# Two sequences transformed inside SBUF instead of one, and full-width transfers in the first stage

## The chip, the cores and the metric

One core of one Trainium2 chip runs the whole program: TensorE (PE) for matmuls and transposes, VectorE (DVE), ScalarE (ACT), GpSimd (POOL), and SyncE (SP), which only issues transfers here. The metric is the device time of one execution in microseconds; lower is better. Runs of the kernel before gave 543.24, 546.17 and 552.6 us.

## What is computed

Eight sequences of 2496 rows and 256 channels pass a real Fourier transform along the rows, are multiplied by a complex filter per frequency and channel, and are transformed back. The 19968 rows that result go to a mixture of eight experts with 80 places each: a row's expert is the one with the largest logit, each expert keeps the 80 rows with the largest gate, and all other output rows are zero.

```python
X = np.fft.rfft(x, axis=1)
y = np.fft.irfft(X * (filt_r + 1j * filt_i)[None], n=2496, axis=1).reshape(19968, 256)
logits = y @ w_gate                       # 8 experts
expert, gate = argmax(logits), softmax(logits)[expert]
for e in range(8):                        # the 80 rows of e with the largest gate
    out[rows_e] = gate[rows_e] * (relu(y[rows_e] @ w1[e]) @ w2[e])
```

## The kernel before, in words

The length is split as 2496 = 39 x 64: row number 64 n1 + n2. **Stage 1** is a transform over n1 (39 points, of which 20 frequencies s are kept, real and imaginary), one small matmul with the table `wf_t`. Three sequences share a matmul: 3 x 39 = 117 partitions go in, 120 come out. Two forms of it exist.

- The **near** form (`stage1_near`, L363) takes one sequence, sequence 0, whose 64 values of n2 are laid into three parts of 22, 22 and 20, one part per block of 39 partitions. Its chunks (`CHUNKS`, six of them, four values of n2 in each part, the last with two) are loaded as three transfers of 39 partitions. It uses x as the stationary side, so the result has channels on partitions; ACT and DVE copy it into a tile `u`, and `turn_near` (L388) transposes it into the form that stage 2 wants. Nothing goes through DRAM.
- The **far** form (`stage1`, L330) takes a trio of sequences, 1 to 3 and then 4 to 6 (`TRIOS`), in 16 chunks of four values of n2. ACT copies the result to `t1` and stores it on its own transfer queue to a DRAM tile `d1`; `load_t2` (L355) reads it back in the other layout, five loads per sequence. Sequence 7, alone, uses the same route with the chunks of the near form and three small stores per chunk. A trio chunk's x is loaded as 112 and 5 partitions.

**Stage 2** (`stage2`, L401) runs in steps: a step is two frequencies s of one sequence, ten steps per sequence, 80 in all. It transforms over n2 (eight instructions on PE with the table `d_t`), DVE multiplies by the two filter planes `ft`, POOL forms the complex sum. Two steps later (`LATE`) `turn` (L424) transposes the result with the gate weights beside it; ACT copies it out, DVE reduces the gate part. Spectra of sequences 0, 1, 2 and 7 stay in SBUF (`KEEP`), the others go to DRAM in `yf`, through a ring of two `ysp` tiles and POOL's queue. The filter planes are loaded as rows (`load_filter`, L280) and transposed on PE (`turn_filter`, L290) in five groups during sequence 0, each group with a part of `d_t`.

The order is written out by hand (from L786): `plan` says after which part of which step a piece runs. `chunk()` runs one stage-1 chunk and first issues the load of the chunk four places on. Before step 0 the six near chunks of sequence 0 run; the first trio's 16 chunks lie in steps 0 to 7, the second trio's in steps 10 to 34, sequence 7's in steps 60 to 65. The loads of `t2` for a sequence stand one sequence ahead, those of sequence 1, 4 and 7 in the last steps. From step 42 on, logits, gating and a first selection (`logits_e`, `logits`, `gating`, `first_pick`) of sequences 0 to 5 are placed in between. SP's queue is in order, and each of its transfers also waits for a free completion slot, of which the eight are used in turn by SP and ACT.

After step 81 come the **rows out**: for each sequence, in the order `ORDER`, the table rows of up to 128 selected positions are gathered (`fetch`), transposed in five groups and multiplied with that sequence's spectrum (`turn_rows`, `rows_out`). Spectra in DRAM are loaded into two buffers (`spectrum`). `aside` places other pieces by group number, 40 groups in all. Then the experts run on the 640 rows. `put_zeros` writes the zeros of the output, 26 transfers in all: in steps 40 to 61, in ten of the groups, and eight in the expert stage, which the planner may place earlier since nothing there is written out by hand.

The stationary table of the far form and its load:

```python
wf_t = tpool.tile([NP1, NM1], F32, name="wf_t")          # 117 x 120
for p0, np_ in ((0, 112), (112, NP1 - 112)):             # load_x, trio
    nc.sync.dma_start(out=xt[p0:p0 + np_], ...)
```

Of the kernel before, what the change touches and what calls it, by code (L numbers as in the profile page):

```python
# [29 lines left out]

H3, J3 = 3, 22
# [3 lines left out]
TRIOS = (1, 4)  # L35
# [11 lines left out]
ORDER = (0, 1, 2, 3, 4, 5, 6, 7)  # L47
# [3 lines left out]
def dft_tables():  # L51
# [27 lines left out]
    return (wf.reshape(NP1, NM1).astype(f32), v.transpose(2, 0, 1).astype(f32),  # L79
# [5 lines left out]
def kernel(  # L85
# [14 lines left out]
    wf_host, wi_host, d_host, e_host, rows_host = dft_tables()  # L100
    wf_dram = nc.inline_tensor(wf_host, name="wf_tbl")
    wi_dram = nc.inline_tensor(wi_host, name="wi_tbl")
# [131 lines left out]
    with ExitStack() as fctx, tc.manual_schedule():  # L234
# [19 lines left out]
        wf_t = tpool.tile([NP1, NM1], F32, name="wf_t")  # L254
# [5 lines left out]
        ft = [tpool.tile([128, NS, NDB, NQ], F32, name=f"ft{i}") for i in range(2)]  # L260
# [3 lines left out]
        def load_tables(part):  # L264
            if part == 0:
                nc.scalar.dma_start(out=wf_t, in_=wf_dram.ap())
# [23 lines left out]
        def turn_filter(k, g):  # L290

            ps = fps.tile([128, SG, NDB, NQ], F32, name=f"pf_{k}_{g}", tag="f")
            for i in range(SG):
                for cb in range(NDB):
                    nc.tensor.transpose(ps[:, i, cb, :],
                                        fst[k, g][0:NQ, i, 128 * cb:128 * cb + 128],
                                        ident[0:NQ, 0:NQ])
            nc.vector.tensor_copy(out=ft[k][:, SG * g:SG * g + SG], in_=ps[:])
# [3 lines left out]
        def load_x(b, ch, trio=False):  # L302
            if trio:
                xt = xpool.tile([128, JC, C], F32, name=f"x_{b}_{ch}", tag="x")
                for p0, np_ in ((0, 112), (112, NP1 - 112)):
                    nc.sync.dma_start(
                        out=xt[p0:p0 + np_],
                        in_=bass.AP(tensor=x.tensor,
                                    offset=x.offset + (b * S + N2 * p0 + JC * ch) * C,
                                    ap=[[N2 * C, np_], [C, JC], [1, C]]))  # L310
                st["x", b, ch] = xt
                return
            j0, jn = CHUNKS[ch]
            xt = xpool.tile([128, JC, C], F32, name=f"x_{b}_{ch}", tag="x")

            def rows(p0, np_, j1, jm, row):
                nc.sync.dma_start(
                    out=xt[p0:p0 + np_, j1:j1 + jm, :],
                    in_=bass.AP(tensor=x.tensor, offset=x.offset + row * C,
                                ap=[[N2 * C, np_], [C, jm], [1, C]]))  # L320

            for h in range(H3):
                r0 = b * S + J3 * h + j0
                if b == B - 1 and h == H3 - 1 and J3 * h + j0 + jn > N2:
                    rows(N1 * h, N1 - 1, 0, jn, r0)
                    rows(N1 * h + N1 - 1, 1, 0, jn, B * S - jn)
                else:
                    rows(N1 * h, N1, 0, jn, r0)
            st["x", b, ch] = xt

        def stage1(b, ch, trio):
# [6 lines left out]
            j0, jn = (JC * ch, JC) if trio else CHUNKS[ch]  # L338
# [7 lines left out]
            if trio:  # L346
                nc.scalar.dma_start(out=st["d1w", b][:, j0:j0 + jn, :], in_=t1[:, 0:jn, :])
                return
            for h in range(H3):
                n0 = J3 * h + j0  # L350
                jm = min(jn, N2 - n0)
                if jm > 0:
# [437 lines left out]
        for b in TRIOS:  # L790
            xs += [(b, ch, True) for ch in range(NTC)]
# [689 lines left out]
```

## Time and profile before

| | |
|---|---|
| median of three runs | 546.17 us (543.24 to 552.6) |
| the profiled execution | 544.47 us, span 542.7 us, mean granted TensorE clock 0.906 |
| PE matmuls | 458.3 us, 84% of the span |
| DVE, POOL, ACT | 202.4, 175.2, 154.6 us |
| moved by DMA | 135.92 MB, mean 250 GB/s |
| queue of SP and ACT (q1, q10) / POOL (q0) | 53.0% and 10.0% / 12.0% of 16 engines |

The span is the time from the first to the last instruction; the 1.8 us beside it lie around the program. Busy shares are means over stages with different limits, so the rows further down are taken by stretch and from the instructions in order of time. A timeline row gives the start, the length, the engine, the line, the operation, how many instructions it merges, and in brackets how long the engine had stood idle and what ended that. A granted clock of 1.00 is 2.4 GHz; a stretch with less is a mean over the two levels, 1.2 and 2.4.

### The profile page before, as it was taken

Reading aid. Unit: us, or ns where it says so; the run is one execution under the profiler, and the core shown is the slowest. Engines: PE = TensorE matmul, PEld = TensorE weight load, DVE = VectorE, ACT = ScalarE, POOL = GpSimd, SP = SyncE. Lnnn points to the kernel's source line nnn. Section 1 sums busy time; section 2 is a strip of 40 time slices with the busy share of each in tenths; the row PEclk is TensorE's granted clock in tenths of the full one; section 3 lists DMA queues with packets and bytes.
Section 4 is the critical chain, followed back from the end, with each engine's and each line's share of the span. In section 5 each row is a group of like instructions: output and inputs, shape, how many; then the busy total and the mean of one; then the engine's idle time right before and its main releaser. Section 6 shows DMA issues by size and latency. Waiting matters only on the chain. (4 is left out here: it accounts for less than half of the span.)

```text
span 542.7 us, 7821 instructions
## 1 busy us (share of the span) xinstructions
PE 458.3 (84%) x2845; PEld 378.6 (70%) x2845; DVE 202.4 (37%) x516; ACT 154.6 (28%) x292; POOL 175.2 (32%) x257
## 2 busy tenths in 40 slices
PE   5397797799999989979977877998998796599993
PEld 5374554678878879868846776876887685588882
DVE  4042312354554544887226897036350000001110
ACT  1133342244444224533344121342322121001110
POOL 4010221344454654577324456011025000401111
PEclk9788989899999989999898897798999888569997
DMA  7978989799989797999943600978558987949400
GB/s 207 202 176 264 286 224 325 233 370 327 332 296 306 239 385 260 374 364 382 324 166 130 229 39 7 403 274 298 175 190 284 401 294 229 337 171 320 169 13 13
DMA packets 71671, 135.92 MB, mean 250 GB/s; under 512 B 5445, under 2 KB 54085, under 8 KB 69961
## 3 DMA queue, kind: packets, MB, share of 16 engines
q1 hardware_dynamic: 60180, 92.98, 53.0%
q0 software_dynamic: 6144, 23.95, 12.0%
q10 hardware_dynamic: 5300, 18.41, 10.0%
q8 instruction: 25, 0.41, 0.3%
q14 instruction: 22, 0.17, 0.1%
HBM read 82.68 MB, written 52.64 MB: 249 GB/s over the span
## 5 line engine op out<-in xcount | busy, mean ns | idle before, releaser
L419 POOL TENSOR_TENSOR yt<-p,p 128x256 f32<-128x256 f32 x80 | 61.2, 764 | 187.8 <-PE py L431 104.5
L414 DVE TENSOR_TENSOR p<-pb,ft 128x512 f32<-128x512 f32 x160 | 102.6, 683 | 22.3 <-PE pb L407 19.7
L431 PEld LDWEIGHTS py<-gi,yt 128*128 128x128 f32 x640 | 88.5, 204 | 26.9 <-issue 15.5
L431 PE MATMUL py<-gi,yt 128*128 128x136 f32 x640 | 95.3, 295 | 11.8 <-POOL yt L421 9.1
L407 PE MATMUL pb<-d_t,t 128*128 128x128 f32 x640 | 90.1, 286 | 3.5 <-DMA t<-d 2.3
L407 PEld LDWEIGHTS pb<-d_t,t 128*128 128x128 f32 x640 | 82.0, 200 | 7.8 <-issue 6.1
L343 PE MATMUL pa<-x,wf_t 117*120 117x512 f32 x150 | 76.8, 643 | 9.3 <-DMA x<-in_x_dram 9.0
L345 ACT COPY t<-pa 120x512 f32<-120x512 f32 x75 | 42.8, 586 | 71.9 <-PE pa L343 51.7
L421 POOL TENSOR_TENSOR yt<-p,p 128x256 f32<-128x256 f32 x80 | 58.8, 735 | 0.0
L456 DVE TENSOR_REDUCE z<-py 128x16 f32<-128x32 f32 x80 | 15.0, 188 | 116.1 <-ACT yk L453 75.5
L343 PEld LDWEIGHTS pa<-x,wf_t 117*120 117x120 f32 x150 | 27.3, 199 | 36.3 <-issue 23.6
L941 PE MATMUL po<-yb,wt 128*128 128x256 f32 x160 | 40.4, 398 | 5.5 <-DMA yb<-yf 4.5
L941 PE MATMUL po<-yk,wt 128*128 128x256 f32 x160 | 39.9, 396 | 1.3 <-ACT wt L929 1.3
L453 ACT COPY ysp<-py 128x512 f32<-128x512 f32 x40 | 23.0, 584 | 62.2 <-DMA yf<-ysp 32.8
L929 ACT COPY wt<-pw 128x512 f32<-128x512 f32 x40 | 23.3, 586 | 55.5 <-PE pw L928 55.3
L941 PEld LDWEIGHTS po<-yb,wt 128*128 128x128 f32 x160 | 30.4, 201 | 9.7 <-issue 4.9
L1060 PEld LDWEIGHTS ph<-xs,w 128*128 128x128 f32 x256 | 36.1, 227 | 1.1 <-DVE xs L1056 0.5
L1060 PE MATMUL ph<-xs,w 128*128 128x80 f32 x256 | 36.1, 311 | 0.3 <-DVE xs L1056 0.3
L453 ACT COPY yk<-py 128x512 f32<-128x512 f32 x40 | 23.4, 585 | 43.8 <-PE py L431 40.3
L941 PEld LDWEIGHTS po<-yk,wt 128*128 128x128 f32 x160 | 30.4, 200 | 5.2 <-ACT wt L929 1.6
L1074 PE MATMUL po<-w,hT 128*80 128x256 f32 x128 | 31.3, 394 | 0.0
L1056 DVE COPY xs<-px 128x160 f32<-128x160 f32 x8 | 2.5, 323 | 72.5 <-PE px L1053 72.5
(164 smaller groups left out, 393.5 us busy)
## 6 DMA issues: line engine op xcount, KB each, us to landing
out_dram<-zero_t SPq DMA_DIRECT2D x26, 768.0 KB
t<-d SPq DMA_DIRECT2D x35, 512.0 KB
w<-in_moe_w_dram SPq DMA_DIRECT2D x16, 1024.0 KB
d<-t ACTq DMA_DIRECT2D x32, 480.0 KB
x<-in_x_dram SPq DMA_DIRECT2D x32, 448.0 KB
yf<-ysp POOLq DMA_DIRECT2D x20, 512.0 KB
yb<-yf SPq DMA_DIRECT2D x4, 2560.0 KB
x<-in_x_dram SPq DMA_DIRECT2D x30, 156.0 KB
```

The source lines that it names most:

```text
L343: nc.tensor.matmul(out=ps[0:NM1], lhsT=wf_t, rhs=xt[0:NP1, 2 * i:2 * i + 2, :], start=True, stop=True)
L345: nc.scalar.copy(out=t1[:, 2 * i:2 * i + 2, :], in_=ps[0:NM1])
L407: nc.tensor.matmul(out=ps[:, i, cb], rhs=d_t[:, s, :], start=True, stop=True, lhsT=st["t2", b, s // SG][:, s % SG, 128 * cb:128 * cb + 128])
L414: nc.vector.tensor_tensor(out=pt, in0=ps[:].rearrange("p s c r q -> p (s c) r q"), in1=f.unsqueeze(2).to_broadcast([128, 2 * NDB, 2, NQ]), ...
L419: nc.gpsimd.tensor_tensor(out=yt[:, :, 0, :], in0=pr[0][:, :, 0, :], in1=pr[1][:, :, 1, :], op=AL.subtract)
L421: nc.gpsimd.tensor_tensor(out=yt[:, :, 1, :], in0=pr[0][:, :, 1, :], in1=pr[1][:, :, 0, :], op=AL.add)
L431: nc.tensor.matmul(out=ps[:, i, 136 * cb:136 * cb + 136], rhs=gi[:, cb, :], lhsT=yt[:, 2 * i + cb].rearrange("p r q -> p (r q)"), start=Tr ...
L453: nc.scalar.copy(out=ys[:, m:m + 2, :].rearrange("p i (k c) -> p i k c", k=NDB), in_=ps[:, :, 0:288].rearrange("p i (k c) -> p i k c", k=N ...
L929: nc.scalar.copy(out=wts[t][:, SG * g:SG * g + SG, :], in_=ps[:])
L941: nc.tensor.matmul(po, lhsT=wts[t][:, s, :], rhs=yk[b][g][:, m, :], start=(s == 0), stop=(s == NS - 1))
L1060: nc.tensor.matmul(ph[:, fc // 4, fc % 4, 0:cap], lhsT=w1s[e][:, k, 128 * fc:128 * fc + 128], rhs=xs[:, k, :], start=(k == 0), stop=(k == ...
L1074: nc.tensor.matmul(po[0:cap, :], lhsT=hT[:, fc, :], rhs=w2s[e][:, fc, :], start=(fc == 0), stop=(fc == NFC - 1))
```

## The change

- Sequences 0 and 1 both take the near form; the trios are 2 to 4 and 5 to 7. The far form for one sequence is gone. The chunks of sequence 1 lie in steps 0 to 5, its transposes (`turn_near`) in steps 9, 11, 13, 15 and 17; the first trio's chunks in steps 5 to 15, the second's in steps 20 to 44.
- The first stage's transfers: a near part takes every third partition (0, 3, ... or 1, 4, ... or 2, 5, ...) with a table `wn_t` in that order. A trio chunk is one load over 128 partitions, whose first eleven belong to the sequence before and meet zero rows in the table (now 128 x 128); the store is 128 partitions wide, into a DRAM tile padded to 64 frequencies.
- Both filter planes are loaded into one tile of 128 partitions and transposed together; a group is 8 transposes of 128 x 128 instead of 16 of 64.
- The start: five chunks ahead instead of four, ahead of the filters and `d_t`; the third part of sequence 0's chunks goes to ACT's queue. A chunk's load is issued after the chunk that frees its buffer.
- Rows out in the order 0, 3, 1, 4, 2, 5, 6, 7, with the loads of spectra 5 and 6 at groups 10 and 20 (20 and 25 before).
- Zeros: 14 in steps 50 to 76, six in the groups, six in the expert stage.

```diff
--- before.py
+++ after.py
...
-TRIOS = (1, 4)
+TRIOS = (2, 5)
...
-ORDER = (0, 1, 2, 3, 4, 5, 6, 7)
+ORDER = (0, 3, 1, 4, 2, 5, 6, 7)
...
-    return (wf.reshape(NP1, NM1).astype(f32), v.transpose(2, 0, 1).astype(f32),
+    wt = np.zeros((128, 128))
+    wt[128 - NP1:, :NM1] = wf.reshape(NP1, NM1)
+    wn = wf.transpose(1, 0, 2, 3, 4).reshape(NP1, NM1)
+    return (wt.astype(f32), wn.astype(f32), v.transpose(2, 0, 1).astype(f32),
...
-        wf_t = tpool.tile([NP1, NM1], F32, name="wf_t")
+        wf_t = tpool.tile([128, 128], F32, name="wf_t")
+        wn_t = tpool.tile([NP1, NM1], F32, name="wn_t")
...
-        ft = [tpool.tile([128, NS, NDB, NQ], F32, name=f"ft{i}") for i in range(2)]
+        ft = tpool.tile([128, 2, NS, NDB, NQ], F32, name="ft")
...
+                nc.scalar.dma_start(out=wn_t, in_=wn_dram.ap())
                 nc.scalar.dma_start(out=wf_t, in_=wf_dram.ap())
...
-        def load_filter(k, g):
-            fst[k, g] = t2pool.tile([128, SG, C], F32, name=f"fst_{k}_{g}", tag="t2")
-            filt = (filt_r, filt_i)[k]
+        def load_filter(g):
+            fst[g] = t2pool.tile([128, SG, C], F32, name=f"fst_{g}", tag="t2")
             for q in range(2):
-                off, step = (0, C) if q == 0 else (N1 * C, -C)
+                for k, filt in enumerate((filt_r, filt_i)):
+                    off, step = (0, C) if q == 0 else (N1 * C, -C)
+                    nc.sync.dma_start(
+                        out=fst[g][64 * k + 32 * q:64 * k + 32 * q + 32],
+                        in_=bass.AP(tensor=filt.tensor, offset=filt.offset + off + step * SG * g,
+                                    ap=[[N1 * C, 32], [step, SG], [1, C]]))
+        def turn_filter(g):
+            for i in range(0, SG, 2):
+                ps = fps.tile([128, 2, NDB, 2, NQ], F32, name=f"pf_{g}_{i}", tag="f")
+                for m in range(2):
+                    for cb in range(NDB):
+                        nc.tensor.transpose(ps[:, m, cb].rearrange("p k q -> p (k q)"),
+                                            fst[g][:, i + m, 128 * cb:128 * cb + 128], ident[:])
+                s = SG * g + i
+                nc.vector.tensor_copy(
+                    out=ft[:, :, s:s + 2].rearrange("p k s c q -> p (s c) k q"),
+                    in_=ps[:].rearrange("p s c k q -> p (s c) k q"))
...
+        def load_x(b, ch, trio):
+            xt = xpool.tile([128, JC, C], F32, name=f"x_{b}_{ch}", tag="x")
+            st["x", b, ch] = xt
+            if trio:
+                row = b * S - N2 * (128 - NP1) + JC * ch
                 nc.sync.dma_start(
-                    out=fst[k, g][32 * q:32 * q + 32],
-                    in_=bass.AP(tensor=filt.tensor, offset=filt.offset + off + step * SG * g,
-                                ap=[[N1 * C, 32], [step, SG], [1, C]]))
...
-        def load_x(b, ch, trio=False):
-            if trio:
-                xt = xpool.tile([128, JC, C], F32, name=f"x_{b}_{ch}", tag="x")
-                for p0, np_ in ((0, 112), (112, NP1 - 112)):
-                for p0, np_ in ((0, 112), (112, NP1 - 112)):
-                    nc.sync.dma_start(
...
             j0, jn = CHUNKS[ch]
-            xt = xpool.tile([128, JC, C], F32, name=f"x_{b}_{ch}", tag="x")
...
-            def rows(p0, np_, j1, jm, row):
...
+            for h in range(H3):
+                row = b * S + J3 * h + j0
+                q = nc.scalar if b == 0 and h == H3 - 1 else nc.sync
+                q.dma_start(
+                    out=xt[h:NP1:H3, 0:jn, :],
                     in_=bass.AP(tensor=x.tensor, offset=x.offset + row * C,
-                                ap=[[N2 * C, np_], [C, jm], [1, C]]))
...
+                                ap=[[N2 * C, N1], [C, jn], [1, C]]))
...
+        def stage1(b, ch):
             if ch == 0:
-                n = H3 if trio else 1
-                d1 = d1pool.tile([n * NS, 2 * N2, C], F32, name=f"d1_{b}")
-                for i in range(n):
+                d1 = d1pool.tile([64, 2 * N2, C], F32, name=f"d1_{b}")
+                d1 = d1pool.tile([64, 2 * N2, C], F32, name=f"d1_{b}")
+                for i in range(H3):
...
-            t1 = t1pool.tile([NM1, JC, C], F32, name=f"t1_{b}_{ch}", tag="t1")
-            for i in range(jn // 2):
+            t1 = t1pool.tile([128, JC, C], F32, name=f"t1_{b}_{ch}", tag="t1")
+            for i in range(JC // 2):
                 ps = fps.tile([128, 2, C], F32, name=f"pa_{b}_{ch}_{i}", tag="f")
-                nc.tensor.matmul(out=ps[0:NM1], lhsT=wf_t, rhs=xt[0:NP1, 2 * i:2 * i + 2, :],
+                nc.tensor.matmul(out=ps, lhsT=wf_t, rhs=xt[:, 2 * i:2 * i + 2, :],
                                  start=True, stop=True)
-                nc.scalar.copy(out=t1[:, 2 * i:2 * i + 2, :], in_=ps[0:NM1])
...
-            for h in range(H3):
-                n0 = J3 * h + j0
-                jm = min(jn, N2 - n0)
-                if jm > 0:
-                    nc.scalar.dma_start(out=st["d1w", b][:, n0:n0 + jm, :],
-                                        in_=t1[2 * NS * h:2 * NS * h + 2 * NS, 0:jm, :])
+                nc.scalar.copy(out=t1[:, 2 * i:2 * i + 2, :], in_=ps)
+            nc.scalar.dma_start(out=st["d1w", b][:, JC * ch:JC * ch + JC, :], in_=t1)
...
-        def stage1_near(ch):
...
-                st["u"] = keep_a.tile([128, NDB, NS, 2, N2], F32, name="u", tag="ka")
-            xt = st.pop(("x", 0, ch))
+                st["u", b] = keep_a.tile([128, NDB, NS, 2, N2], F32, name=f"u_{b}", tag="ka")
+            xt = st.pop(("x", b, ch))
...
-                                     lhsT=xt[0:NP1, j, 128 * cb:128 * cb + 128], rhs=wf_t,
+                                     lhsT=xt[0:NP1, j, 128 * cb:128 * cb + 128], rhs=wn_t,
...
-        def turn_near(g):
-            t2 = t2pool.tile([128, SG, C], F32, name=f"t2_0_{g}", tag="t2")
-            u = st["u"].rearrange("p k s r n -> p k s (r n)")
+        def turn_near(b, g):
+            t2 = t2pool.tile([128, SG, C], F32, name=f"t2_{b}_{g}", tag="t2")
+            u = st["u", b].rearrange("p k s r n -> p k s (r n)")
...
-        xs = [(0, ch, False) for ch in range(len(CHUNKS))]
+        todo = [(b, ch, False) for b in range(TRIOS[0]) for ch in range(len(CHUNKS))]
         for b in TRIOS:
-            xs += [(b, ch, True) for ch in range(NTC)]
-        xs += [(B - 1, ch, False) for ch in range(len(CHUNKS))]
-        todo = list(xs)
+            todo += [(b, ch, True) for ch in range(NTC)]
+        NX1 = 5
         def chunk():
-            if len(todo) > 4:
-                load_x(*todo[4])
-            b, ch, trio = todo.pop(0)
-            if b == 0:
-                stage1_near(ch)
+            b, ch, trio = todo[0]
+            if trio:
+                stage1(b, ch)
             else:
-                stage1(b, ch, trio)
-
-        for i in range(4):
+                stage1_near(b, ch)
+            if len(todo) > NX1:
+                load_x(*todo[NX1])
+            todo.pop(0)
+        for i in range(NX1):
             load_x(*todo[i])
-        load_d(0)
         for t in range(B, B + NX):
             nc.gpsimd.dma_start(out=y_sel[128 * t:128 * t + 128, :], in_=zero_t[:, 0:C])
         def ahead(g):
             if g < NS // SG:
-                if g:
-                    load_d(g)
-                for k in range(2):
-                    load_filter(k, g)
+                load_filter(g)
+                load_d(g)
...
+        for i in range(len(CHUNKS)):
+            put(i, 1, chunk)
         for i in range(NTC):
-            put(i // 2, 1, chunk)
-            put(NU + 25 * i // NTC, 1, chunk)
-        for i in range(len(CHUNKS)):
-            put(NU * NA + i, 1, chunk)
-
-        for b in range(1, B):
+            put(5 + 11 * i // NTC, 1, chunk)
+        for i in range(NTC):
+            put(2 * NU + 26 * i // NTC, 1, chunk)
+        for g in range(NS // SG):
+            put(NU - 1 + 2 * g, 2, part(turn_near, 1, g))
+        for b in range(2, B):
             for g in range(NS // SG):
-                u = 8 + (g > 2) if b == 1 else 2 * g
-                if b in (TRIOS[1], B - 1):
-                    u = 7 + (g > 2) + (g > 3)
-                put(NU * (b - 1) + u, 2, part(load_t2, b, g))
+                put(NU * (b - 1) + (8 + (g > 2) if b in TRIOS else 2 * g), 2, part(load_t2, b, g))
...
-        for i in range(8):
-            put(NU * 4 + 3 * i, 2, part(put_zeros, 1))
+        for i in range(14):
+            put(NU * 5 + 2 * i, 2, part(put_zeros, 1))
         ahead(0)
+        chunk()
         ahead(1)
-        for ch in range(len(CHUNKS)):
+        for ch in range(1, len(CHUNKS)):
             chunk()
         for g in range(NS // SG):
-            turn_near(g)
-            for k in range(2):
-                turn_filter(k, g)
+            turn_near(0, g)
+            turn_filter(g)
             ahead(g + 2)
             step(2 * g)
             step(2 * g + 1)
...
-        aside.setdefault(20, []).append(lambda: spectrum(5))
-        aside.setdefault(25, []).append(lambda: spectrum(6))
+        aside.setdefault(20, []).append(lambda: spectrum(6))
+        aside.setdefault(10, []).append(lambda: spectrum(5))
         aside.setdefault(30, []).append(lambda: load_weights(0))
         aside.setdefault(35, []).append(lambda: load_weights(1))
-        for i in range(10):
-            aside.setdefault(4 * i + 1, []).append(lambda: put_zeros(1))
+        for i in (3, 7, 12, 15, 22, 26):
+            aside.setdefault(i, []).append(lambda: put_zeros(1))
...
-        put_zeros(3 if e < 4 else NZ)
+        put_zeros(2 if e < 4 else NZ)
```

## Rows read from the trace of the kernel before

**Rows 1.** Windows: stretch, its us, PE PEld DVE ACT POOL busy, PEclk, DMA share, GB/s.
```profile
6.00:30.00 24.00, 14.96 (x87) 14.68 (x88) 4.83 (x20) 3.42 (x15) 0.53 (x2) 0.82 0.96 222
30.00:108.00 78.00, 64.26 (x338) 42.46 (x337) 23.91 (x44) 25.98 (x47) 14.08 (x20) 0.90 0.83 251
108.00:190.00 82.00, 81.46 (x537) 65.48 (x537) 41.75 (x86) 34.63 (x60) 41.27 (x60) 1.00 0.95 312
253.00:291.00 38.00, 34.30 (x194) 25.48 (x194) 12.34 (x30) 15.35 (x29) 11.47 (x18) 0.87 0.67 235
340.00:360.00 20.00, 19.69 (x116) 16.09 (x116) 0.95 (x2) 7.49 (x14) 0.61 (x1) 0.83 0.99 400
```

**Rows 2.** Timeline, SP then PE, start: start us, us, engine, line, operation.
```profile
16.84 4.25 SPq L317 DMA_DIRECT2D x<-in_x_dram  x6
...
14.65 2.02 PE L372 MATMUL pn<-wf_t,x 117*128 117x120 f32 x16 [0.63 <-DMA x<-in_x_dram]
...
24.99 5.45 PE L372 MATMUL pn<-wf_t,x 117*128 117x120 f32 x24 [8.33 <-DMA x<-in_x_dram]
...
33.21 1.16 PE L407 MATMUL pb<-d_t,t 128*128 128x128 f32 x8
```

**Rows 3.** Timeline of PE, steps 4 and 8.
```profile
67.00 6.39 PE L343 MATMUL pa<-x,wf_t 117*120 117x512 f32 x8 [3.10 <-DMA x<-in_x_dram]
...
99.37 1.69 PE L407 MATMUL pb<-d_t,t 128*128 128x128 f32 x8 [1.17 <-DVE t L396]
```

**Rows 4.** Timeline of PE at the full clock, single kinds of work.
```profile
79.40 1.04 PE L393 MATMUL pt<-ident,u 128*128 128x128 f32 x8
...
170.44 1.88 PE L343 MATMUL pa<-x,wf_t 117*120 117x512 f32 x4
...
180.26 1.05 PE L407 MATMUL pb<-d_t,t 128*128 128x128 f32 x8
...
182.08 1.05 PE L407 MATMUL pb<-d_t,t 128*128 128x128 f32 x8
```

**Rows 5.** Timeline of PE, stage 2 of steps 10, 40, 50, 60, 70.
```profile
107.20 1.13 PE L407 MATMUL pb<-d_t,t 128*128 128x128 f32 x8 [2.31 <-DMA t<-d]
...
190.33 1.05 PE L407 MATMUL pb<-d_t,t 128*128 128x128 f32 x8
...
222.78 1.06 PE L407 MATMUL pb<-d_t,t 128*128 128x128 f32 x8
...
253.18 1.05 PE L407 MATMUL pb<-d_t,t 128*128 128x128 f32 x8
...
305.22 2.08 PE L407 MATMUL pb<-d_t,t 128*128 128x128 f32 x8
```

**Rows 6.** The page's DMA issues: what, queue, count, KB of each.
```profile
out_dram<-zero_t SPq DMA_DIRECT2D x26, 768.0 KB
...
t<-d SPq DMA_DIRECT2D x35, 512.0 KB
...
d<-t ACTq DMA_DIRECT2D x32, 480.0 KB
...
x<-in_x_dram SPq DMA_DIRECT2D x32, 448.0 KB
...
yf<-ysp POOLq DMA_DIRECT2D x20, 512.0 KB
...
x<-in_x_dram SPq DMA_DIRECT2D x30, 156.0 KB
```

**Rows 7.** Timeline of ACT and its queue, steps 40 and 62.
```profile
193.10 1.07 ACT L453 COPY ysp<-py 128x512 f32<-128x512 f32 x2 [6.38 <-DMA yf<-ysp]
...
265.78 3.84 ACTq L353 DMA_DIRECT2D d<-t  x3
```

**Rows 8.** Busy time by stretch, steps 56 to 61.
```profile
240.00:260.00 20.00, 16.23 (x104) 13.87 (x103) 15.85 (x37) 7.26 (x14) 14.31 (x21) 0.91 1.04 372
```

**Rows 9.** Timeline of PE in the rows-out stage.
```profile
432.20 3.75 PE L941 MATMUL po<-yb,wt 128*128 128x256 f32 x8 [3.90 <-DMA yb<-yf]
```

More of the change, by code (lines that the diff above doesn't have):

```diff
@@ L98 @@
     assert 1 <= cap <= 128
-    wf_host, wi_host, d_host, e_host, rows_host = dft_tables()
+    wf_host, wn_host, wi_host, d_host, e_host, rows_host = dft_tables()
     wf_dram = nc.inline_tensor(wf_host, name="wf_tbl")
+    wn_dram = nc.inline_tensor(wn_host, name="wn_tbl")
     wi_dram = nc.inline_tensor(wi_host, name="wi_tbl")
@@ L290, in turn_filter @@
[L290 to L298, printed above, removed]
-        st, zt = {}, {}
-        def load_x(b, ch, trio=False):
-            if trio:
-                xt = xpool.tile([128, JC, C], F32, name=f"x_{b}_{ch}", tag="x")
-                for p0, np_ in ((0, 112), (112, NP1 - 112)):
-                    nc.sync.dma_start(
[L307 to L311, printed above, removed]
+                for k, filt in enumerate((filt_r, filt_i)):
[4 more added lines that the diff above has]
+                                    ap=[[N1 * C, 32], [step, SG], [1, C]]))
@@ L312, in load_x @@
+        st, zt = {}, {}
+        def load_x(b, ch, trio):
[3 more added lines that the diff above has]
+                row = b * S - N2 * (128 - NP1) + JC * ch
+                nc.sync.dma_start(
+                    out=xt, in_=bass.AP(tensor=x.tensor, offset=x.offset + row * C,
+                                        ap=[[N2 * C, 128], [C, JC], [1, C]]))
                 return
             j0, jn = CHUNKS[ch]
-            xt = xpool.tile([128, JC, C], F32, name=f"x_{b}_{ch}", tag="x")
@@ L316, in rows @@
-            def rows(p0, np_, j1, jm, row):
-                nc.sync.dma_start(
-                    out=xt[p0:p0 + np_, j1:j1 + jm, :],
-                    in_=bass.AP(tensor=x.tensor, offset=x.offset + row * C,
-                                ap=[[N2 * C, np_], [C, jm], [1, C]]))
-            for h in range(H3):
[L323 to L328, printed above, removed]
@@ L344, in stage1 @@
                                  start=True, stop=True)
-                nc.scalar.copy(out=t1[:, 2 * i:2 * i + 2, :], in_=ps[0:NM1])
[L346 to L349, printed above, removed]
-                n0 = J3 * h + j0
-                jm = min(jn, N2 - n0)
-                if jm > 0:
-                    nc.scalar.dma_start(out=st["d1w", b][:, n0:n0 + jm, :],
-                                        in_=t1[2 * NS * h:2 * NS * h + 2 * NS, 0:jm, :])
+                nc.scalar.copy(out=t1[:, 2 * i:2 * i + 2, :], in_=ps)
@@ L381, in stage1_near @@
                         n0 = J3 * h + j0
-                        copy(out=st["u"][:, cb, :, :, n0:n0 + jm].rearrange(
+                        copy(out=st["u", b][:, cb, :, :, n0:n0 + jm].rearrange(
                                  "p s r j -> p (s r) j"),
                              in_=ps[:, 0:jm, h].rearrange("p j s r -> p (s r) j"))
-        def turn_near(g):
-            t2 = t2pool.tile([128, SG, C], F32, name=f"t2_0_{g}", tag="t2")
-            u = st["u"].rearrange("p k s r n -> p k s (r n)")
+        def turn_near(b, g):
+            t2 = t2pool.tile([128, SG, C], F32, name=f"t2_{b}_{g}", tag="t2")
+            u = st["u", b].rearrange("p k s r n -> p k s (r n)")
             for i in range(0, SG, 2):
-                ps = fps.tile([128, 2, C], F32, name=f"pt_{g}_{i}", tag="f")
+                ps = fps.tile([128, 2, C], F32, name=f"pt_{b}_{g}_{i}", tag="f")
                 for m in range(2):
@@ L396, in turn_near @@
                 copy(out=t2[:, i:i + 2, :], in_=ps[:])
-            st["t2", 0, g] = t2
+            st["t2", b, g] = t2
         NU = NS // 2
@@ L412, in stage2 @@
                 pt = ppool.tile([128, 2 * NDB, 2, NQ], F32, name=f"p{k}_{b}_{u}", tag=f"p{k}")
-                f = ft[k][:, 2 * u:2 * u + 2].rearrange("p s c q -> p (s c) q")
+                f = ft[:, k, 2 * u:2 * u + 2].rearrange("p s c q -> p (s c) q")
                 nc.vector.tensor_tensor(
```

6 lines of the change are left out of this document (2 added, 4 removed).

## The prediction

> **What bounds the kernel now.** I read the stretches first, then TensorE's instructions in order of time, then the transfers. TensorE (PE) is the engine that every stage passes through, and the table of stretches shows where it isn't fed: busy 15.0 of 24 us in 6 to 30, 64.3 of 78 in 30 to 108, but 81.5 of 82 in 108 to 190 [rows 1]. In the first two the 16 DMA engines show a share of 0.96 and 0.83 while they move only 222 and 251 GB/s; in 340 to 360 the same share moves 400 [rows 1]. So the front (near stage of sequence 0, and steps 0 to 9) is held by loads, the middle by PE. What the reader should see in the start: SyncE (SP) issues the fifth x chunk at 16.84, behind filters and tables in its queue, and PE stands 8.33 us until 24.99 [rows 2]. In steps 0 to 9 the same happens in small, 3.10 us before the row at 67.00, and the eight matmuls behind it take 6.39 us on the lower of the clock's two levels (1.2 for 2.4 GHz; 0.90 granted on the mean of 30 to 108, 1.00 at 108 to 190) [rows 1, 3]; four at the upper level take 1.88 [rows 4]. Step marks are the rows of stage 2: step 0 at 33.21 [rows 2], 10 at 107.20, 40 at 190.33, 50 at 222.78, 60 at 253.18, 70 at 305.22 [rows 5].
>
> **Prices on PE at full clock.** A bare step (stage 2 and a turn) is 182.08 - 180.26 = 1.82 us; a trio chunk is 1.88, of which 0.17 lies under the next instruction (its neighbours' overlap), so 1.71; eight 128-wide transposes 1.04 [rows 4]; sixteen near instructions 2.02, so the 88 of a sequence at most 11.1, and 10 taken [rows 2].
>
> **The start.** The new order puts five x chunks ahead of the filters, one third on ACT's queue. The 8.33 wait goes, and the 24 instructions behind it run at the pace of the sixteen (3.0 us for 5.45): -10.7. Late next is the sixth chunk, behind the first filters and d_t group: some 3.5 MB (15 loads of 156 KB, tables, one filter and table group of 0.8 MB, three small loads), 12 to 16 us at 300 to 222 GB/s from about 3 us on. That is 15 to 19, when PE is at its fifth chunk, so at worst 2 us stay. ACT issues seven transfers before its first copy; its queue is held for some 4 us while it has nothing to copy. Taken: -10, ends -8 and -11; step 0 at 23.
>
> **Steps 0 to 9** (74.0 us now). Half of the first trio's chunks leave; the second near stage comes. PE work: 16.4 (nine full steps' worth, as the first two have no turn), 8 chunks 13.7, near 10, six groups of near transposes 6.2, five filter groups 5.2 (eight wide transposes each in place of sixteen narrow ones; DVE's ten copies keep their size): 51.5. For x still late I add 4, between 0 and the excess of now: that is 74 less the work of the present plan, 16.4 + 16 x 1.71 + 5 x 1.04 twice, so 20. Four is taken since the bytes ask for less: 13 trio chunks of 0.52 MB, 8 stores of 0.52, x of sequence 1 at 2.5, three filter and table groups 2.4, together 16 MB [rows 6], 288 GB/s over 55.5 us. -19; ends -22 and -10. DVE and ACT gain six near chunks' copies; they are busy 24 and 26 of 78 us in this stretch [rows 1], so these lie beside PE (without that cover some 0.9 us per chunk).
>
> **Steps 10 to 39** (83.1 now). 30 x 1.82 = 54.6, 21 chunks 35.9, four near transposes 4.2. The near t2 of sequence 1 is made right ahead of the step that uses it; the same pattern shows 1.17 us of waiting on DVE's copy [rows 3], five times 5.9 (between 0 and 1.3 each). Sum 100.6: +17.5. Load here: 19 x chunks, 21 stores, 15 t2 loads, four yf stores of 0.52 MB and one 1.3 MB table, 32.3 MB, 321 GB/s; 108 to 190 moved 312 at a share of 0.95 [rows 1, 6]. So transfers and PE are about level: at 312 it would be 103.5 (+20), at 400 PE alone is left.
>
> **What the wider transfers give.** Each trio load becomes one of 512 KB over 128 partitions for 448 and 20 KB, each store 512 for 480 [rows 6]: 2.4 MB more in all. The near loads are spread in steps of three partitions. The nearest rows for their pace are 222 GB/s (39 neighbouring partitions each) and 400 (full width) [rows 1]; I take 300 to 330. The Trainium skill (SBUF — State Buffer, "Door 1: The DMA port swizzle") says that a transfer's bandwidth follows how many of 16 ports its partitions reach; 39 neighbours reach about half of them, the step of three all, and the 222 beside 400 agrees. Against the change speaks a rule of DMA: Bandwidth & Descriptors ("Why a DMA increments its semaphore by 16 and not by 1"): the split goes over the largest divisor up to 16, so 39 partitions use 13 engines. By that, near loads stop at 13/16 of 400, 325 GB/s, and 5 MB take 3 us more than at full width; no row here shows it alone.
>
> **Steps 40 to 49** (32.4 now): three chunks come, 5.1; the first zero write moves away from step 40, where ACT waited 6.38 us for a yf store [rows 7] and PE lost about 4. +1, ends -3 and +5. **Steps 50 to 59** (30.4): DVE is busy 15.9 of 20 us there [rows 8] with gating and products; untouched, 0.
>
> **Steps 60 to 69** (52.0 now). Sequence 7's own first stage goes: 11 matmuls of 512 columns, 5.5 chunks, 9.4 us; 17 stores on ACT's queue (by the loop), of which three held its queue 3.84 us [rows 7] with the turn's and the logits' copies behind them; PE idled 3.7 of 38 us there and its clock was granted at 0.87 [rows 1], some 5 us lost. So -9.4 at least, -18 at most. Late next is DVE's gating chain of sequences 4 and 5. -14.
>
> **Zeros.** All 26 writes of 768 KB [rows 6] stay; fourteen now lie in steps 50 to 76, and the planner may set the tail's six beside them. With yf and t2 of these steps that is 26 MB in about 80 us, 325 GB/s: hidden by DVE's steps while the yf stores keep their share; t2 behind them on SP has ten steps of room. 0, between -3 and +10 (rival two).
>
> **Rows out.** The order 0, 3, 1, 4, 2 frees the two buffers of loaded spectra earlier, so the loads of 5 and 6 start about 10 and 5 groups sooner. The 3.90 us wait for yb goes, and the eight matmuls behind it take 1.9 for 3.75 [rows 9]: -6. Spectrum 3 is needed about 15 us after its load starts, 5 MB ahead of or beside it at 400 GB/s: 13 us, hidden barely; if not, +2. The tail of experts is unchanged.
>
> **Sum:** -10 - 19 + 17.5 + 1 - 14 - 6 = -30.5 from the profiled execution's 544.47 us (span 542.7): 514. The median of the runs is 546.17, 1.7 above it: **515.5** for a median.
>
> **Rivals.** One: the full width moves no more than the present one, and the front stays bound by transfers at the 251 GB/s of now throughout. Then steps 0 to 9 take 16/0.251 = 64 and 10 to 39 32.3/0.251 = 129 us: 37 over my sum, 552, no change. For it: the share of 0.83 to 0.96 in the whole front; against it: 312 with the same kinds of transfer at 108 to 190 [rows 1]. At 290 GB/s it is 525, inside my range. 0.12. Two: zeros queued with yf make ACT wait for its yf buffer, as at 193 [rows 7]; if half of the ten stores of sequences 5 and 6 cost 4 us, or if the planner sets the tail's six zeros (4.7 MB, 15 us) in steps 20 to 39, it is +15 to +20, about 533. 0.08. Three, slower: loads onto every third partition run row by row. 36 of them carry 5.7 MB, all before step 6; to eat 31 us and another 11 they must take 42 us more than the 19 of 300 GB/s, so it decides below 93 GB/s; at 70 it is 81 us, 575. Nothing in the trace shows such a load; against it, the rows of 4 KB are as long as before. 0.05. Four: a tie by several small losses, 0.07.
>
> **Chances.** The forecast has 0.68 and 499 to 527. Faster by over 2% (below 535; about what a measurement of this kernel can tell from no change): 0.68, half of two (0.04), a third of one, at paces over 275 GB/s (0.04), and over half of four (0.04), 0.80. Slower: three and 0.02 of the ends of one and four, 0.07. Within: 0.13. The range leaves out 2 in 10: 498 to 535.
>
> **What would show it.** Right: no PE wait over 2 us for x before step 0, and step 0 near 23, step 10 near 79, step 40 near 179, 60 near 243, 70 near 281; first stretch above 280 GB/s. Wrong: x rows with waits as at 67.00 still through steps 0 to 9 (the four added microseconds), PE short of busy at 10 to 39 (rival one), ACT's yf waits in steps 50 to 70 (rival two), a near stage that ends after 31 us (rival three).

## The result, and the profile after

The changed kernel took **520.05 us** (median of four runs, 518.33 to 528.97) beside 544.70 (541.28 to 552.6) for the kernel before: ratio 0.9546, interval 0.9478 to 0.9613. It is faster, by 24.65 us where 30.7 were forecast (515.5 from 546.17). Run once more beside its variants it took 523.2 for 549.85, ratio 0.9605 (0.950 to 0.971). Some executions are disturbed and run longer at a lower granted clock: the ratios leave them out, so 0.9605 is not 523.2 / 549.85, and as the one profiled first was such a one, the profile shown is of the second set: 524.25 us, span 522.4.

Step marks are the starts of stage 2, as in the forecast; the forecast column is its own term added to the stage before. All are us of the profiled executions.

| stage | before | forecast | after | t1 of three, zeros late |
|---|---|---|---|---|
| to step 0 | 33.2 | 23 | 22.7 | 24.8 |
| steps 0 to 9 | 74.0 | 55 | 59.1 | 49.7 |
| 10 to 19 / 20 to 39 | 30.3 / 52.8 | 100.6 together | 48.3 / 58.7 | 39.7 / 58.7 |
| 40 to 49 | 32.4 | 33.4 | 32.8 | 32.8 |
| 50 to 59 | 30.4 | 30.4 | 31.3 | 30.4 |
| 60 to 69 | 52.0 | 38 | 39.1 | 39.1 |
| 70 to the first transposed rows | 39.3 | 39.3 | 39.2 | 38.6 |
| rows out, to the experts' first layer | 123.9 | 117.9 | 116.9 | 114.2 |
| experts, to the end | 74.3 | 74.3 | 74.3 | 74.0 |
| span | 542.7 | 512.2 | 522.4 | 502.0 |

The same stretches of after by busy time (stretch, its us, busy us of PE, PEld, DVE, ACT and POOL with their instructions, granted clock, DMA share, GB/s) answer to [rows 1, 8]; the first is the near stage, the others go from mark to mark.

```profile
6.00:20.00 14.00, 11.54 (x85) 11.42 (x86) 6.35 (x39) 4.70 (x16) 0.55 (x2) 1.00 0.85 264
...
22.72:81.81 59.09, 50.70 (x338) 41.53 (x337) 27.55 (x60) 20.30 (x46) 14.12 (x20) 0.97 0.88 296
81.81:130.07 48.26, 41.53 (x225) 30.54 (x225) 16.57 (x33) 16.61 (x29) 12.32 (x18) 0.89 0.85 295
130.07:188.79 58.72, 58.72 (x375) 46.29 (x374) 30.20 (x62) 26.96 (x46) 30.16 (x44) 1.00 0.99 334
...
221.61:252.92 31.31, 26.47 (x195) 24.01 (x194) 27.50 (x62) 12.55 (x24) 22.65 (x33) 0.89 0.93 316
252.92:292.03 39.11, 33.16 (x241) 29.80 (x239) 22.35 (x54) 12.79 (x24) 20.34 (x32) 0.87 0.75 257
```

Steps 20 to 39 are filled by PE to the last hundredth, at 334 GB/s. Steps 10 to 19 are not: 6.7 of 48.3 us idle, the clock at 0.89, and the transfers at a share of 0.85. So neither engine nor bytes are the bound there, and a wait has to be looked for. The start, by PE's timeline (start, length; in brackets the idle time before and what ended it), answers to [rows 2]: eighty near instructions run through, and the one wait after the first is 1.05; one of the five filter groups lies before the mark of step 0, and the first near instructions of sequence 1 wait 1.59 for x.

```profile
7.40 11.00 PE L362 MATMUL pn<-wn_t,x 117*128 117x120 f32 x80 [7.40 <-DMA x<-in_x_dram]
19.46 1.12 PE L362 MATMUL pn<-wn_t,x 117*128 117x120 f32 x8 [1.05 <-DMA x<-in_x_dram]
...
21.84 1.04 PE L303 MATMUL pf<-ident,fst 128*128 128x128 f32 x8
22.72 1.06 PE L397 MATMUL pb<-d_t,t 128*128 128x128 f32 x8
25.36 2.02 PE L362 MATMUL pn<-wn_t,x 117*128 117x120 f32 x16 [1.59 <-DMA x<-in_x_dram]
```

All engines around step 7, in order of time:

```profile
60.10 0.33 ACTq L344 DMA_DIRECT2D d<-t  x1
...
65.20 1.37 SPq L216 DMA_DIRECT2D out_dram<-zero_t  x2
65.22 1.07 ACT L343 COPY t<-pa 128x512 f32<-128x512 f32 x2 [5.15 <-DMA d<-t]
...
65.86 1.97 PE L303 MATMUL pf<-ident,fst 128*128 128x128 f32 x8 [2.90 <-ACT t L343]
...
67.31 0.19 DVE L446 TENSOR_REDUCE z<-py 128x16 f32<-128x32 f32 x1 [8.48 <-ACT yk L443]
```

ACT stands 5.15 us before its copy into `t1`, which has two buffers, until a store has read one of them. Behind it in ACT's order are the copy of the turn (`yk`) and half of the `t2` copy; DVE's reduction waits for the first, and DVE's half of `t2` stands behind that. The two zero writes between are of the expert stage: the planner, free to place that stage's six, issued them at 65 to 93 us (two, one, one, two), among the trio's loads. PE pays in the stage 2 that reads `t2`, which answers to [rows 3, 4]:

```profile
81.81 1.13 PE L397 MATMUL pb<-d_t,t 128*128 128x128 f32 x8 [3.19 <-DVE t L386]
82.78 3.46 PE L341 MATMUL pa<-x,wf_t 128*128 128x512 f32 x4
...
95.89 1.41 PE L397 MATMUL pb<-d_t,t 128*128 128x128 f32 x8 [2.48 <-DVE t L386]
97.09 3.34 PE L341 MATMUL pa<-x,wf_t 128*128 128x512 f32 x4
...
110.22 2.02 PE L397 MATMUL pb<-d_t,t 128*128 128x128 f32 x8 [2.74 <-DVE t L386]
112.03 2.69 PE L341 MATMUL pa<-x,wf_t 128*128 128x512 f32 x4
...
116.38 1.88 PE L341 MATMUL pa<-x,wf_t 128*128 128x512 f32 x4
```

Five such waits, in steps 10, 12, 14, 16 and 18, make 9.9 us (the two not shown are 0.8 and 0.7; the first ends at the mark of step 10 and so counts in steps 0 to 9), and the chunk after the three long ones runs wholly or partly at the clock's lower level (granted 0.52, 0.56 and 0.70): 3.46, 3.34 and 2.69 for 1.88, 3.85 us more.

### The profile page after: what moved, and what is told of

It reads as the page before. It is cut to its first block, busy times and chain, and to the rows that moved or that the text cites. A ratio compares the mean times of both kernels' runs of the same rounds, so it can differ in the third digit from the quotient of the medians.

```text
span 527.2 us, 7948 instructions
## 1 busy us (share of the span) xinstructions
PE 457.6 (87%) x2911; PEld 387.2 (73%) x2911; DVE 207.9 (39%) x538; ACT 155.8 (30%) x303; POOL 175.7 (33%) x257
## 5 line engine op out<-in xcount | busy, mean ns | idle before, releaser
L421 PEld LDWEIGHTS py<-gi,yt 128*128 128x128 f32 x640 | 85.4, 197 | 29.0 <-POOL yt L411 15.2
L421 PE MATMUL py<-gi,yt 128*128 128x136 f32 x640 | 91.9, 288 | 12.7 <-POOL yt L411 12.0
L397 PE MATMUL pb<-d_t,t 128*128 128x128 f32 x640 | 92.5, 291 | 10.4 <-DVE t L386 9.3
L397 PEld LDWEIGHTS pb<-d_t,t 128*128 128x128 f32 x640 | 83.8, 204 | 15.1 <-ACT t L386 11.0
L341 PE MATMUL pa<-x,wf_t 128*128 128x512 f32 x128 | 65.0, 640 | 0.0
L411 POOL TENSOR_TENSOR yt<-p,p 128x256 f32<-128x256 f32 x80 | 59.1, 738 | 0.0
L343 ACT COPY t<-pa 128x512 f32<-128x512 f32 x64 | 36.7, 587 | 62.6 <-PE pa L341 47.4
L928 PE MATMUL po<-yk,wt 128*128 128x256 f32 x160 | 38.2, 383 | 1.3 <-ACT wt L916 1.3
L341 PEld LDWEIGHTS pa<-x,wf_t 128*128 128x128 f32 x128 | 24.4, 209 | 19.9 <-issue 15.8
L928 PE MATMUL po<-yb,wt 128*128 128x256 f32 x160 | 37.8, 379 | 0.0
L1047 PEld LDWEIGHTS ph<-xs,w 128*128 128x128 f32 x256 | 36.1, 227 | 0.9 <-DVE xs L1043 0.4
L1047 PE MATMUL ph<-xs,w 128*128 128x80 f32 x256 | 36.1, 311 | 0.1
L362 PE MATMUL pn<-wn_t,x 117*128 117x120 f32 x176 | 24.6, 304 | 9.5 <-DMA x<-in_x_dram 9.5
```

The lines of the kernel that those rows point to most:

```text
L341: nc.tensor.matmul(out=ps, lhsT=wf_t, rhs=xt[:, 2 * i:2 * i + 2, :], start=True, stop=True)
L343: nc.scalar.copy(out=t1[:, 2 * i:2 * i + 2, :], in_=ps)
L362: nc.tensor.matmul(out=ps[:, j].rearrange("p h s r -> p (h s r)"), lhsT=xt[0:NP1, j, 128 * cb:128 * cb + 128], rhs=wn_t, start=True, stop= ...
L397: nc.tensor.matmul(out=ps[:, i, cb], rhs=d_t[:, s, :], start=True, stop=True, lhsT=st["t2", b, s // SG][:, s % SG, 128 * cb:128 * cb + 128])
L411: nc.gpsimd.tensor_tensor(out=yt[:, :, 1, :], in0=pr[0][:, :, 1, :], in1=pr[1][:, :, 0, :], op=AL.add)
L421: nc.tensor.matmul(out=ps[:, i, 136 * cb:136 * cb + 136], rhs=gi[:, cb, :], lhsT=yt[:, 2 * i + cb].rearrange("p r q -> p (r q)"), start=Tr ...
```

## The experiments

Eleven kernels, the first unedited, each of the others the changed one with the edit shown. They ran in three sets on three chips, the kernel before beside each. The re-run, three buffers, zeros late and neighbouring partitions are one set and compare in us; across sets the ratio to the kernel before (in brackets, with its interval) is the measure. Executions differ where nothing was edited. Step 0 lies at 22.5 to 24.8 us in the profiles that share the start's code, and steps 0 to 19 take 103.8 to 111.4 in the five whose code there is the changed kernel's or differs in the start or the near loads alone. So a gain read there against the 107.4 of the re-run is good to some 4 us. An edit is read from its own stage first.

**The changed kernel again.** 

> The changed kernel as it is, for the others of this set to stand beside. It should take 520 us (518 to 523), 0.955 of the kernel before. If the two-buffer theory below holds, ScalarE's copy into t1 waits for the store of d some five times in steps 6 to 18, 10 us or more in sum, and the four matmuls behind some of these waits take some 3 us for 1.88.

523.2 us, 0.9605. ACT's waits for the store are 7.5 us in two, where some five, with 10 us or more in sum, were expected; two more (2.96 and 2.50) the profile puts down to PE's transposes, though the matmuls they copy were over before. TensorE's side is as expected.

**Three buffers for `t1`.**

```diff
-        t1pool = pool("t1", 2, stack=actx)
+        t1pool = pool("t1", 3, stack=actx)
```

The tile `s2` of sequences 0 to 5 becomes one of these buffers, and, outside steps 0 to 19, the one-hot tile `bplc` gets three buffers for two.

> The changed kernel with three buffers for t1 in place of two (to make room, the logits' small tile of sequences 0 to 5 shares them). Theory A (in steps 6 to 18 ScalarE stands before its copy into t1 until a store has left the buffer, t2's copy behind it is late, TensorE stands and its clock falls): ScalarE's waits for the store fall from some 13 us to under 4, steps 10 to 19 from 49.5 to 43 us or less, the whole 6 to 12 us shorter, 508 to 514. Theory C (the sixteen DMA engines are full there and stand for any buffer): the wait only moves to x or t2, within 2 us of the changed kernel.

514.75 us (0.9431, 0.928 to 0.958). Steps 0 to 19 take 100.7 for 107.4, but 6.1 of it in steps 0 to 9; steps 10 to 19, where theory A had its gain, only fell from 48.3 to 47.7. No wait for a store is left, and one large wait has come. ACT and its queue, before stage 2 of step 12:

```profile
83.93 1.07 ACT L343 COPY t<-pa 128x512 f32<-128x512 f32 x2 [1.15 <-PE pa L341]
89.86 0.33 ACTq L344 DMA_DIRECT2D d<-t  x1
90.22 0.58 ACT L443 COPY yk<-py 128x512 f32<-128x512 f32 x1 [5.22 <-DMA e_t<-e_tbl]
```

PE's stage 2 behind it, and then the busy time of the stretch:

```profile
91.78 2.04 PE L397 MATMUL pb<-d_t,t 128*128 128x128 f32 x8 [6.10 <-DVE t L386]
```

```profile
82.00:90.00 8.00, 3.67 (x21) 2.48 (x19) 0.00 (x0) 1.66 (x3) 1.41 (x2) 1.00 1.02 412
```

ACT issues the next store 4.86 us after its copies, and the profile names the landing of `e_t`, 1.3 MB, issued at 75.89. So by the profile ACT's queue waits for a completion slot that `e_t` holds, while the transfers move 412 GB/s at a full share. A is right on the buffer, then, and C on what stands behind it once the buffer is there.

**The tail's zeros late.**

```diff
+        for i in range(6):
+            put(NU * 7 + 6 + i, 2, part(put_zeros, 1))
...
-        put_zeros(2 if e < 4 else NZ)
```

> The changed kernel with the six zero writes of the tail given fixed places at steps 76 to 81, so that none lies among the trio's transfers in steps 6 to 12. Theory B (these 4.7 MB make the stores late): 4 to 10 us shorter, 510 to 516, with step 20 some 5 to 9 us earlier and ScalarE's waits for the store under 6 us in sum although t1 has two buffers. Theory A alone (the third buffer is what lacks): within 3 us of the changed kernel. Against both: the zeros behind step 75 delay the rows out, up to 6 us longer.

514.59 us (0.9464, 0.936 to 0.957). Steps 0 to 19 take 99.8 us, step 20 starts 7.3 earlier, the rows out are no later. The mechanism came half as expected: ACT still waits for stores, 12.1 us in five (the first, 4.78, is the 5.15 above, which ended as the first zero write was issued and so can't be the zeros'), but TensorE's waits for `t2` fall to 6.4 us, none above 1.72, and in steps 10 to 19 the clock stays up:

```profile
79.91:122.82 42.91, 36.75 (x224) 27.89 (x225) 16.56 (x33) 16.51 (x29) 12.34 (x18) 1.00 0.82 278
```

**Both.** The two edits together.

> Both edits at once: three buffers for t1, and the tail's six zero writes at steps 76 to 81. Apart, the first took 6 us from steps 0 to 9 and 1 from 10 to 19, the second 2 and 5. If they take different waits (the buffer, and a DMA queue so full that the issue of a store or load holds its engine, as 4.8 us on ScalarE and 4.55 us on SyncE at 82 to 90 us of the run with three buffers), steps 0 to 19 take some 93 us for 107, the whole 12 to 15 us less than the changed kernel. If both only feed the same wait, 100 us as with either, the whole 8 to 9 less.

506.76 us (0.9272, 0.920 to 0.935). Steps 0 to 19 take 89.3, 18.0 less than the changed kernel, for 6.6 and 7.5 of the two apart; had both fed the same wait, some 100 would be left. So the two work on different waits. The five waits for `t2` are all 0.7 to 0.9 now (PE's timeline, two of them), and the clock is at 1.00 (the stretches of steps 0 to 9 and 10 to 19):

```profile
85.15 1.13 PE L397 MATMUL pb<-d_t,t 128*128 128x128 f32 x8 [0.78 <-DVE t L386]
...
95.94 1.13 PE L397 MATMUL pb<-d_t,t 128*128 128x128 f32 x8 [0.89 <-DVE t L386]
```

```profile
24.82:74.47 49.65, 48.48 (x338) 40.18 (x337) 27.27 (x60) 20.69 (x46) 14.14 (x20) 1.00 0.89 285
74.47:114.13 39.66, 36.49 (x225) 27.98 (x226) 16.59 (x33) 17.00 (x29) 12.34 (x18) 1.00 0.91 311
```

My expectation's "queue so full" was a guess at the cause; the profile's row says `e_t`'s slot. Here `e_t` has the same place in the program (issued at 72.2 us) and, with the zeros away, no store is late: the slot alone is not the cost.

**The near transposes a step earlier, alone.**

```diff
-            put(NU - 1 + 2 * g, 2, part(turn_near, 1, g))
+            put(NU - 2 + 2 * g, 2, part(turn_near, 1, g))
```

> The changed kernel with the near transposes of sequence 1 one step earlier and nothing else; t1 keeps its two buffers, the zeros their places. If the five late copies of t2 (9 to 10 us of TensorE's waiting in sum, and the clock behind them) have a cost of their own: 5 to 9 us less, 512 to 516. If they are only where the late stores show: the wait moves to the x chunks or to another stage 2, within 3 us of the changed kernel.

517.4 us (0.9532, 0.936 to 0.971): not separable from the changed kernel as a whole. Steps 0 to 19 take 97.8, the next twenty 1.8 more than 58.7. ACT now waits for stores in nine places, 22.2 us in sum, and PE before its transposes (2.05 and 1.35 the longest) and, ahead of step 20, 3.51 for the far `t2`: distance hides the wait, it does not remove it. Still, though ACT waits longer than in the re-run (22.2 us for 7.5), the front is 9.6 shorter, no less than by either edit before (6.6 and 7.5). So what a wait of ACT costs hangs on how soon PE needs what stands behind it.

**Four edits.** Both, the transposes earlier, and the load of `e_t` from step 9 to step 30.

```diff
-            if g == NS // SG - 1:
-                load_tables(2)
...
+        put(NU * 3, 2, part(load_tables, 2))
```

> Both edits, and two more: the near transposes of sequence 1 one step earlier, so that DVE's and ScalarE's copies to t2 are done before the stage 2 that reads them, and the load of the 1.3 MB table e_t from step 9 to step 30. If the waits for t2 (0.7 to 3 us, five of them) are cured by distance, TensorE waits for t2 under 1 us in sum in steps 9 to 18 and steps 0 to 19 take 4 to 6 us less than with both edits alone, some 88 us. If the copies are held by ScalarE's own queue (its store issue), the wait only moves to the step before: within 2 us.

**500.97 us** (0.9138, 0.907 to 0.921): faster than either kernel. Steps 0 to 19 take 86.7, 2.6 less than with two edits where 4 to 6 were expected; no wait for near `t2` is left. The rest of the 5.8 us between the medians is not tied to a stage: the profile is of the longest of the five executions, 508.39 us, and from step 70 to the first transposed rows it takes 47.6 us for 38.6 with two edits, in code that is the same.

**Narrow trio transfers**, in the changed kernel and in the version with four edits: loads of 112 and 5 partitions, stores of 120 rows, table and `d1` to match.

```diff
-                row = b * S - N2 * (128 - NP1) + JC * ch
-                nc.sync.dma_start(
+                for p0, np_ in ((0, 112), (112, NP1 - 112)):
+                    nc.sync.dma_start(
+                        out=xt[p0:p0 + np_],
...
```

> The changed kernel with the trio loads as in the kernel before (112 and 5 partitions, 448 and 20 KB) and stores of 120 rows; all else stays. If the one full-width transfer moves more than the pair: steps 10 to 19 get 3 us or more longer and the waits for stores and x grow, the whole 3 to 10 us longer, 525 to 533. If the full width brings nothing: the 2.4 MB less are within 2 us of the changed kernel, either way.

> The version with all four edits, and with the narrow trio transfers (112 and 5 partitions, stores of 120 rows). With the waits of steps 0 to 19 gone there is room for what the transfers' width is worth: if full width is faster, 3 us or more longer than the 501 with full width; if not, within 2 us, 499 to 503, with steps 0 to 19 at 87 us either way.

516.78 us (0.9474, 0.939 to 0.956), steps 0 to 19 at 101.8; and 503.19 (0.9303, 0.916 to 0.944), at 88.1 for 86.7. The full width of the trio's transfers gives nothing that these runs can measure. The changed kernel with narrow ones is, if anything, some 2 us ahead there; whether that is the 2.4 MB less stays open. The profile of the version with four edits and narrow transfers shows a front without holes (steps 10 to 19 by busy time) and, at step 20, a wait for far `t2` (PE's timeline; 1.37 there with full width):

```profile
74.48:110.86 36.38, 35.61 (x226) 27.56 (x225) 17.50 (x35) 18.17 (x31) 14.31 (x21) 1.00 0.89 289
```

```profile
110.86 1.16 PE L399 MATMUL pb<-d_t,t 128*128 128x128 f32 x8 [0.77 <-DMA t<-d]
```

**Near loads on neighbouring partitions.**

```diff
-    wn = wf.transpose(1, 0, 2, 3, 4).reshape(NP1, NM1)
+    wn = wf.reshape(NP1, NM1)
...
-                    out=xt[h:NP1:H3, 0:jn, :],
+                    out=xt[N1 * h:N1 * h + N1, 0:jn, :],
```

> The changed kernel with the near loads on blocks of 39 neighbouring partitions, as in the kernel before; order, queues and sizes of all transfers stay. If the spread over every third partition gives the start its speed: waits of 3 us or more for x come back in the near stage, step 0 at 27 to 33 for some 22.5, the whole 5 to 10 us longer, 525 to 530. If the order of the transfers alone did it: step 0 within 1 us of the changed kernel, and the whole too.

523.16 us (0.9601, 0.947 to 0.973), the same as the changed kernel. Step 0 at 24.2 lies inside the spread of the unedited start, and the largest wait for x ahead of it is small (PE's timeline, then the near stage by busy time):

```profile
20.96 1.12 PE L362 MATMUL pn<-wn_t,x 117*128 117x120 f32 x8 [1.75 <-DMA x<-in_x_dram]
```

```profile
6.00:20.00 14.00, 12.02 (x80) 11.87 (x80) 6.45 (x39) 4.70 (x16) 0.53 (x1) 1.00 0.89 241
```

241 GB/s stand against 254 to 266 in six profiles with the changed kernel's start and spread loads, about 8% under them. The Trainium skill (SBUF — State Buffer, "Door 1: The DMA port swizzle") lets a transfer's bandwidth follow the ports that it reaches. By that, an estimate, a single transfer of 39 neighbours would have about half. In this stretch, where other transfers run beside the near loads, the trace shows 8% and no time that can be told apart; no row has near loads alone.

**The old start.**

```diff
-                q = nc.scalar if b == 0 and h == H3 - 1 else nc.sync
+                q = nc.sync
...
-        for i in range(NX1):
+        for i in range(NX1 - 1):
...
-        chunk()
         ahead(1)
-        for ch in range(1, len(CHUNKS)):
+        load_x(*todo[NX1 - 1])
+        for ch in range(0, len(CHUNKS)):
```

> The changed kernel with the start as before: only four x chunks ahead of the filters, tables and filters of two groups ahead of the fifth, all x loads on SyncE's queue. Loads stay on every third partition. If the order makes the gain of the start: the wait before the fifth chunk comes back (6 to 9 us), step 0 at 30 to 33 for some 22.7, the whole 6 to 10 us longer, 526 to 530. If steps 0 to 9 catch up, since they are bound by the transfers anyway: step 10 within 3 us of the changed kernel's 82, the whole within 3.

526.26 us (0.9709, 0.954 to 0.987). The wait for the fifth chunk is back:

```profile
21.73 5.24 PE L362 MATMUL pn<-wn_t,x 117*128 117x120 f32 x24 [5.62 <-DMA x<-in_x_dram]
```

Step 0 comes at 29.1, 6.4 later (4 to 7 by the spread above), and step 20 at 134.3, where the four other kernels with that front have 126.9 to 133.8. So order, fifth chunk and ACT's queue together are worth some 6 of the start's 10.5; what is left of it by step 20 can't be told from the spread, and the whole, 0.9709 for 0.9605, lies within the intervals. The other 4.1 us of the start were not split. The near stage moves 257 GB/s with the old order and spread loads, where the kernel before, with neighbours, had 225 (the same stretch, this run first):

```profile
6.00:20.00 14.00, 9.43 (x64) 8.97 (x64) 3.66 (x15) 2.73 (x12) 0.54 (x2) 0.99 0.89 257
```

```profile
6.00:20.00 14.00, 9.95 (x64) 9.64 (x64) 3.66 (x15) 2.73 (x12) 0.53 (x2) 1.00 0.96 225
```

**The old order of the rows out.**

```diff
-ORDER = (0, 3, 1, 4, 2, 5, 6, 7)
+ORDER = (0, 1, 2, 3, 4, 5, 6, 7)
```

with the spectra 5 and 6 back at groups 20 and 25.

> The changed kernel with the rows out in the order 0 to 7 and the spectra 5 and 6 loaded from groups 20 and 25. If the order makes the gain there: the wait for yb of 3 to 4 us comes back, and the stretch from the first transposed rows to the experts' first layer takes some 123 us for 114, the whole 6 to 10 us longer, 526 to 530. If the gain there is only that the zeros lie elsewhere: within 2 us of the changed kernel. The steps before stay as they are.

526.61 us (0.966, 0.956 to 0.976), as a whole within the intervals of 0.9605. The stretch takes 119.7 us beside 112.4 to 116.9 in the other profiles of this set of variants: 3 to 7 us are the order's, the rest of the way to 123.9 is not. Two waits are back, for spectrum and gathered rows:

```profile
397.39 1.97 PE L928 MATMUL po<-yb,wt 128*128 128x256 f32 x8 [1.64 <-DMA yb<-yf]
...
410.97 0.83 PE L915 MATMUL pw<-ident,gt 128*128 128x128 f32 x4 [5.12 <-DMA gt<-rows_tbl,idxb]
```

## Why the prediction was right, and where its sum was not

The sign and the bulk of the size were right. In the profiled spans the sum stood at -30.5 and -20.3 came; two terms make all of the 10.2 between them (4.1 and 6.4; the others nearly cancel).

- **Start**: -10 forecast, -10.5 measured. The 8.33 us wait went. Order, fifth chunk and ACT's queue carry some 6 of it.
- **Steps 0 to 9**: -19 forecast, -14.9 measured. The step that failed is "x still late I add 4". The excess is about 10 (59.1 less 48.8, the 49.7 of both edits without their 0.9 us wait), so the lateness was 6 too low. The work of 51.5 was some 2.7 too high, 2.1 of it because one of the six near groups and one of the five filter groups lie before the mark of step 0; that the two errors partly cancel is luck. Of the lateness only 1.6 was x: 6.1 us (2.90 and 3.19) PE stood behind ACT before `t1`, which no part of the sum mentions. I compared bytes with the stretch (288 GB/s) and took buffers and queue order to follow.
- **Steps 10 to 39**: +17.5 forecast, +23.9 measured. Steps 20 to 39 came at 58.72 for the 58.6 of twenty bare steps and thirteen chunks, so the prices on PE and "transfers and PE about level" hold there. Steps 10 to 19 should then have been 42.0 and took 48.3. The step that failed is the "1.17 us of waiting on DVE's copy, five times 5.9". It took the row of before [rows 3] for the pattern's price, but that held only with a free ACT: with both edits the five are 4.1 in sum. With ACT held they are 9.9 (6.7 of it in steps 10 to 19), and the sum has no term for the clock behind them: PE needs 41.5 us in steps 10 to 19 for work of 36.1, 3.85 of the difference in three chunks.
- **The zeros**: the text had the planner set the tail's six in steps 20 to 39, as half of rival two at +15 to +20. They went to steps 7 to 11, and moving them away gave 7.5 us, give or take the 4 above. That half of the rival happened inside the forecast, at another place and half its price.
- **40 to 59**: +0.4 and +0.9, for +1 and 0. **60 to 69**: -12.9 for -14. What of it is PE's 9.4 us and what ACT's queue was not tested by a run; nor does any run take back the near form of sequence 1 or the joint filter tile. **Rows out**: -7.0 for -6; the wait of 3.90 us [rows 9] is gone, and the changed kernel's first loaded spectra are there in time.
- **What the wider transfers give**: no term of the sum stood on width alone, but the text leaned on 222 beside 400 GB/s as a matter of partitions. Two kernels with narrow transfers and one with neighbouring partitions show no time of it. The rate does follow the partitions in part: with the new start neighbours move 241 GB/s and spread loads 254 to 266. And the queue's order alone doesn't make the low rate of before: in the same stretch it was 225 there, and is 257 with the old start and spread loads (the joint filter tile differs too). But none comes near 400, so the agreement that the text saw in 222 beside 400 isn't the partitions' alone; what else makes that difference was not tested. Rival one (the front bound at 251 GB/s) and rival three (loads by rows) are excluded by 296 GB/s in steps 0 to 9 and a near stage done by 21 us. The text's sign of rival one, PE short of busy behind step 10, came all the same, at a DMA share of 0.85: it did not tell a full queue from a held engine.

## What to carry to other kernels

When a stage's bytes and its engine come out level, the next question is not the mean rate but who stands in order behind a transfer: count the buffers between the copy and its store, and follow what is queued behind that copy on the same engine. A wait read from one row is a price only while the engines in its chain are as free as in that row. And whatever a planner may move freely should be given a place when transfers are removed elsewhere, since here it filled the hole that was meant for the tight stage.

## What the runs showed of the hardware

At a share near 1.0 transfers moved 412 GB/s with PE half idle (82 to 90 us, three buffers) and 334 with PE fully busy (steps 20 to 39); the mixes differ (127 of 733 packets under 2 KB, and 6839 of 10047), so neither is a rate of full-width transfers as such. A short wait cost more than itself: after 3.19 us of idle PE four matmuls took 3.46 us for 1.88, after waits of 0.7 to 0.9 us (both edits) the clock stayed at 1.00. And ScalarE stood 4.86 us before it issued a store, its copies into `t1` done, until by the profile an unrelated load of 1.3 MB had landed.
